# Moving operands of the MLP and of one score product begin past a 256-byte boundary

## The chip, the cores and the metric

The kernel runs on one core of a Trainium2 chip, in one launch. The metric is the device time of that core in microseconds (us), the median of three runs.

## The reference, cut to what matters

Three parts follow each other. Attention without softmax on 8 batches of 3072 rows, an MLP with `h - tanh(h)`, and a top-1 mixture of 8 experts over all 24,576 rows:

```python
scores = (1.0 / S) * np.matmul(z, z.transpose(0, 2, 1))   # z: 8 x 3072 x 64
attn = np.maximum(scores, 0.0) ** 2
x = (u * np.matmul(attn, v)).reshape(B * S, D)            # D = 256
h = x @ w_in                                              # 256 x 2048
x = (h - np.tanh(h)) @ w_out                              # 2048 x 256
logits = x @ w_gate                                       # 8 experts, argmax picks one per row
out[mask] = gate_w * eom * (np.maximum(x[mask] @ w1[e], 0.0) @ w2[e])
```

All data is float32.

## The kernel before, in words

Every float32 operand is split into a rounded part (dtype `float32r`, `fp32r` in the profile) and the rest, so that a product takes three matmuls: high by high, low by high, high by low. A matmul reads a moving operand (here mostly 128 partitions x 512 columns, 2048 bytes of each partition) past a weight block of 128 x 128 that an instruction of its own, LDWEIGHTS, has loaded. Every matmul here has its own LDWEIGHTS, loaded while the matmul before it runs.

The 24,576 rows are worked in 48 chunks of 512 rows. In the attention and MLP stage, three things of three chunks run interleaved in an order that is written out by hand (`at(time, function, ...)` puts a task at a due time, `flush` sorts them, and each engine gets its instructions in that order):

- Scores of chunk c (`s_mm`, 12 steps of 4 matmuls). `t1` holds z transposed, the rounded part in partitions 0 to 63 and the rest in 64 to 127; `t4` is the same with the halves swapped, made by two DMAs from `t1` on SP's queue (`t4_make`, lines 299 to 305). Line 347 multiplies by `t1` as moving operand, line 348 by `t4`; the weights are slices of `t1` in both.
- Attention times v (`av_mm`, lines 382 to 384): the moving operand is `a`, the weights are slices of `v`.
- The MLP of an earlier chunk: `wi_mm` (line 412) has `x` as moving operand and slices of `ws` as weights; `g_first`, `g_second` and `g_third` make `g` from its result; `wo_mm` (lines 451 to 453) has `g` as moving operand and other slices of `ws` as weights. `x` is written once a chunk by `x_make` (lines 391, 392), `g` eight times a chunk by lines 438 and 439. The tile `g` also carries the weights of the MLP while they are split at the start (`w_hi`, `w_lo`).

Then comes the expert stage (`w1_mm` line 851, `w2_mm` lines 889 to 900), whose moving operands are `xt` and `b1`.

Tiles lie in SBUF in pools, in the order in which the pools are opened, and in a pool in the order in which the tags are first met; each tile begins at the next multiple of 32 bytes. In the program before, `x` begins at byte 53248 of each partition, the two buffers of `g` at 63488 and 71680, the two of `t4` at 149504 and 151552, `ws`, `v`, `t1`, `a`, `xt`, `b0`, `b1` and `hh` likewise at multiples of 256; within a tile the halves and slices that a matmul reads begin at multiples of 512. One larger tile does not begin on such a boundary: `rows` begins at 22080, which is 64 bytes past one. It is lent to the splitting of the MLP's weights (`w_conv`, lines 238 to 243, and `w_hi`, line 247) for the even ones of eight steps; the odd ones use the tile `x2`, at 45056, a multiple of 256. Both are named `wk`. The last pool of the attention stage ends at 228352 bytes. At its end the stage's pools close, and the pools `c2` and `c3` of the expert stage take their place.

Of the kernel before, what the change touches and what calls it, by code (L numbers as in the profile page):

```python
# [6 lines left out]
F32R = mybir.dt.float32r  # L7
# [10 lines left out]
P = 128  # L18
FLOOR = 2.0**-15
CH = 512  # L20
# [42 lines left out]
def build(tc, u, v, z, w_in, w_out, w_gate, w_ogate, w1, w2, out):  # L63
# [86 lines left out]
    with ExitStack() as st:  # L150
# [3 lines left out]
        p1, p2, p3 = sp("p1", 1), sp("p2", 2), sp("p3", 3)  # L154
        pva = sp("pva", 1)
        ps_s, ps_h, ps_a, ps_x = pp("ps_s", 1), pp("ps_h", 1), pp("ps_a", 1), pp("ps_x", 1)
        pair = lambda pool, tag, name: pool.tile([P, 2, CH], F32, tag=tag, name=name)

        KEEP = (NG, 0, 1, 2)
# [7 lines left out]
        sa = lambda name, bufs: att.enter_context(tc.tile_pool(name=name, bufs=bufs))  # L167
        a1, a2 = sa("a1", 1), sa("a2", 2)
        pvb, pt, a3 = sa("pvb", 1), sa("pt", NG + 1), sa("a3", 3)

        def fills(zero):

            half = TBL // P // 2
            fill = p1.tile([P, 2, 2, CH], F32R, tag="x2", name="fill").bitcast(I32)
            fill = fill.rearrange("p a d f -> p (a d f)")[:, 0:half]
            nc.gpsimd.memset(fill, N)
            tf = table.rearrange("(p k) o -> p (k o)", p=P)
            for h in range(2):
                nc.sync.dma_start(tf[:, h * half : (h + 1) * half], fill)

            for r in range(N - (2 * CH if NA else 0), N + P, P):
                nc.sync.dma_start(x2d[r : r + P, :], zero)
# [60 lines left out]
            stt(ki, L, 29, ki, op0=ALU.logical_shift_right, op1=ALU.bitwise_or)  # L243

        def w_hi(fp):
            hl = p2.tile([P, 2, 2, CH], F32R, tag="g", name="whl")
            nc.scalar.activation(hl[:, :, 0], WS["k", fp], AF.Copy)
            WS["hl", fp] = hl

# [49 lines left out]

        def t4_make(c):  # L300
            t1 = T1[divmod(c, NG)]
            t4 = a2.tile([P, CH], F32R, tag="t4", name="t4")
            nc.sync.dma_start(t4[0:64, :].bitcast(F32), t1[64:128, :].bitcast(F32))
            nc.sync.dma_start(t4[64:128, :].bitcast(F32), t1[0:64, :].bitcast(F32))
            T4[c] = t4
# [80 lines left out]
        def x_make(c):  # L386
            xf = UT.pop(c)
            for d in range(2):
                nc.vector.tensor_mul(xf[:, d], AVP[c][d], xf[:, d])
            x = p1.tile([P, 2, 2, CH], F32R, tag="x", name="x")  # L390
            nc.scalar.activation(x[:, 0], xf, AF.Copy)
            nc.vector.tensor_sub(x[:, 1], xf, x[:, 0].bitcast(F32))  # L392
            X[c] = x
            del AVP[c]
# [38 lines left out]
        def g_third(c, f):  # L433
            d, s, q, m = HH.pop((c, f))
            nc.vector.scalar_tensor_tensor(q, s, pk, q, op0=ALU.add, op1=ALU.mult)  # L435
            nc.vector.copy_predicated(q, m.bitcast(U16), d)  # L436
            gg = p2.tile([P, 2, 2, CH], F32R, tag="g", name="g")
            nc.vector.tensor_copy(gg[:, 0], q)  # L438
            nc.vector.tensor_sub(gg[:, 1], q, gg[:, 0].bitcast(F32))  # L439
            GG[c, f] = gg  # L440
# [160 lines left out]
        for fp in range(NFP):  # L601
            t = K["C0"] + K["C1"] * fp
            at(t - K["WL"], w_load, fp, 0)
            at(t - K["WL"], w_load, fp, 1)
            for which in range(2):
                at(t + which * K["C1"] / 2, w_conv, fp, which)
            at(t + K["CA"], w_hi, fp)
            at(t + K["CP"], w_lo, fp)
# [5 lines left out]
        for c in range(NCH):  # L614
            t0 = c * TC
            at(t0 - (14 if c else 45), t4_make, c)
            at(t0 + TC / 4, u_load, c)
            at(gap(c, K["UT"] * NJP // 12), u_tr, c)
            for p in range(NJP):
# [4 lines left out]
                at(t + LA, av_mm, c, p)  # L624
            end = c == NCH - 1
            at(t0 + TC + LA + 3.0 + K["XM"] if end else t0 + (TC - DJ) + LA + 3.0, x_make, c)
            tm0 = t0 + TC + LA + K["M0"]
            for f in range(NFP):
                t = tm0 + f * DF
                at(t - 22, ws_load, c, f)  # L630
                for i in range(2):
                    at(t + i * K["HI"], wi_mm, c, f, i)
                    lag = K["LG"] * DF + i * K["HI"]
                    if c == NCH - 2 and f == NFP - 1:

                        lag = tm0 + TC + K["W7"] + 0.1 * i - t
                    at(t + lag, wo_mm, c, f, i)
                at(t + K["HI"] + 1.5, g_first, c, f)
                at(t + K["HI"] + K["G2"], g_second, c, f)
                at(t + K["HI"] + K["G3"], g_third, c, f)  # L640
# [5 lines left out]
            n = int((te + 4.0 - EX - t0) // DJ) + 1  # L646
# [349 lines left out]
        n = nc.values_load(nhb[0:1, 0:1], min_val=0, max_val=NHB)  # L996
# [30 lines left out]
```

## Time and profile before

| | us |
|---|---|
| median of three runs | 5693.54 (5691.28 to 5694.91) |
| the profiled execution | 5712.59 |
| its span, first to last instruction | 5710.8 |

The profile is of one execution. PE is TensorE's matmuls, PEld its weight loads, which run beside them; DVE, ACT and POOL are the vector, scalar and GpSimd engines, SP the engine that issues most DMAs. A matmul's recorded duration (0.39 us for 512 columns) holds the time until its result is out, and the next one begins long before that; how fast matmuls follow each other is read from their start times. The granted clock is a share of the full 2.4 GHz.

### The profile page before, as it was taken

The page shows a single profiled execution, that of the slowest core. Times are in us where ns is not written, and L with a number is a line of the kernel's source. Part 1 is how long each engine was busy: PE and PEld are TensorE (multiplying, and loading weights), DVE is VectorE, ACT ScalarE, POOL GpSimd, SP SyncE. Part 2 cuts the span into 40 slices and gives each one's busy share as a digit, 9 for nine tenths or more (in the row PEclk, how much of TensorE's full clock was granted, in tenths as well). Part 3 has the DMA queues.
Part 4 walks back from the last instruction along what each step waited for, and adds up shares of the span by engine and source line. Part 5 has one row for each costly group of instructions (what it writes and reads, how often), then busy time and mean ns, then how long its engine had stood idle before and what let it go on. Part 6 is the DMA issues. An engine that isn't in the chain of part 4 may idle for free. (4 is left out here: it accounts for less than half of the span.)

```text
span 5710.8 us, 70891 instructions
## 1 busy us (share of the span) xinstructions
PE 5603.9 (98%) x26788; PEld 4644.6 (81%) x26788; DVE 4214.3 (74%) x5091; ACT 3570.7 (63%) x3927; POOL 1795.4 (31%) x1169
## 2 busy tenths in 40 slices
PE   7999999999999999999999999999999999999999
PEld 5888888788888888888888888888887888888898
DVE  7888888888888888888888888888888533333344
ACT  5767776777777777677767776777766422222344
POOL 2224222332333233223322332242222233333355
PEclk9999999999999999999999999999999999999999
DMA  5333333333433333343333433343333566666688
GB/s 203 106 128 135 121 130 123 141 127 125 134 127 125 124 136 125 130 129 136 125 127 120 140 127 122 125 143 111 105 112 118 208 228 224 224 223 224 217 293 288
DMA packets 194007, 872.05 MB, mean 153 GB/s; under 512 B 37178, under 2 KB 78272, under 8 KB 130176
## 3 DMA queue, kind: packets, MB, share of 16 engines
q1 hardware_dynamic: 158080, 769.87, 39.3%
q0 software_dynamic: 35584, 97.63, 4.9%
q8 instruction: 213, 3.49, 0.3%
q14 instruction: 130, 1.06, 0.1%
HBM read 757.16 MB, written 98.96 MB: 150 GB/s over the span
## 5 line engine op out<-in xcount | busy, mean ns | idle before, releaser
L367 POOL TENSOR_TENSOR a<-r,a 128x1024 fp32r<-128x1024 f32 x328 | 789.1, 2406 | 2608.9 <-DVE a L364 2608.5
L353 ACT ACTIVATE r<-sc 128x1024 f32<-128x1024 f32 x576 | 587.2, 1019 | 943.3 <-PE sc L348 936.3
L412 PE MATMUL h<-x,ws 128*128 128x512 f32 x4608 | 1157.5, 391 | 15.8 <-DVE x L392 8.1
L412 PEld LDWEIGHTS h<-x,ws 128*128 128x128 f32 x4608 | 860.4, 188 | 199.5 <-DVE x L392 11.5
L383 PE MATMUL av<-a,v 128*128 128x512 f32 x2304 | 903.8, 392 | 12.2 <-DVE a L367 8.0
L382 PE MATMUL av<-a,v 128*128 128x512 f32 x2304 | 905.1, 393 | 2.1 <-ACT a L362 1.1
L384 PE MATMUL av<-a,v 128*128 128x512 f32 x2304 | 901.2, 391 | 0.0
L863 DVE SCALAR_TENSOR_TENSOR hh<-h,hh 128x1024 fp32r<-128x1024 f32 (+1 forms) x248 | 254.7, 1027 | 722.6 <-ACT hh L862 589.8
L862 ACT ACTIVATE hh<-h 128x1024 fp32r<-128x1024 f32 (+1 forms) x248 | 215.2, 868 | 745.3 <-PE h L851 594.4
L851 PE MATMUL h<-xt,b 128*128 128x512 f32 (+1 forms) x2976 | 610.8, 354 | 20.1 <-DVE xt L834 15.9
L354 ACT ACTIVATE r<-r 128x1024 f32<-128x1024 f32 x576 | 611.4, 1061 | 18.3
L452 PE MATMUL x<-g,ws 128*128 128x512 f32 x1536 | 606.5, 395 | 9.9 <-DVE g L439 7.9
L451 PE MATMUL x<-g,ws 128*128 128x512 f32 x1536 | 606.0, 395 | 6.1 <-DVE g L438 6.1
L420 DVE TENSOR_TENSOR gd<-h,gd 128x1024 f32<-128x1024 f32 x384 | 468.9, 1221 | 180.1 <-ACT gs L419 177.2
L453 PE MATMUL x<-g,ws 128*128 128x512 f32 x1536 | 600.7, 391 | 0.0
L851 PEld LDWEIGHTS h<-xt,b 128*128 128x128 f32 x2976 | 478.6, 188 | 113.7 <-DVE xt L834 27.5
L435 DVE SCALAR_TENSOR_TENSOR gq<-gt,gq 128x1024 f32<-128x1024 f32 x384 | 517.8, 1349 | 52.6 <-ACT gt L430 28.3
L364 DVE CAST a<-r 128x1024 fp32r<-128x1024 f32 x470 | 336.9, 717 | 289.3 <-ACT r L354 177.3
L436 DVE COPY_PREDICATED gq<-gm,gd 128x1024 f32<-128x1024 uint16 x384 | 518.9, 1351 | 13.2
L383 PEld LDWEIGHTS av<-a,v 128*128 128x128 f32 x2304 | 435.7, 189 | 105.6 <-DVE a L367 11.4
L382 PEld LDWEIGHTS av<-a,v 128*128 128x128 f32 x2304 | 435.5, 189 | 95.4 <-ACT a L362 3.5
L384 PEld LDWEIGHTS av<-a,v 128*128 128x128 f32 x2304 | 435.4, 189 | 91.8
(154 smaller groups left out, 9930.8 us busy)
## 6 DMA issues: line engine op xcount, KB each, us to landing
ws<-wsd SPq DMA_DIRECT2D x384, 1024.0 KB
b<-wsp SPq DMA_DIRECT2D x102, 2048.0 KB
wsp<-el POOLq DMA_DIRECT2D x32, 1024.0 KB
x2d<-rows SPq DMA_DIRECT2D x48, 576.0 KB
wr<-in_moe_w SPq DMA_DIRECT2D x25, 1024.0 KB
vr<-in_v SPq DMA_DIRECT2D x48, 512.0 KB
ur<-in_u SPq DMA_DIRECT2D x48, 512.0 KB
er<-in_moe_w SPq DMA_DIRECT2D x32, 512.0 KB
```

The lines of the kernel that those rows point to most:

```text
L353: nc.scalar.activation(r, RR.pop((c, p)), AF.Relu, scale=1.0 / S)
L354: nc.scalar.activation(r, r, AF.Square)
L367: eng.tensor_tensor(a[:, 1], r, a[:, 0].bitcast(F32), op=ALU.subtract)
L382: nc.tensor.matmul(dst, vh, a[:, 0, k], start=(J == 0), stop=False)
L383: nc.tensor.matmul(dst, vh, a[:, 1, k], start=False, stop=False)
L384: nc.tensor.matmul(dst, vl, a[:, 0, k], start=False, stop=(J == 2 * NJP - 1))
L412: nc.tensor.matmul(ps, w, xx, start=(n == 0), stop=(n == 5))
L436: nc.vector.copy_predicated(q, m.bitcast(U16), d)
L451: nc.tensor.matmul(dst, wh, gg[:, 0, i], start=first, stop=False)
L452: nc.tensor.matmul(dst, wh, gg[:, 1, i], start=False, stop=False)
L453: nc.tensor.matmul(dst, wl, gg[:, 0, i], start=False, stop=last)
L851: nc.tensor.matmul(ps[:, j], w, xx, start=(n == 0 and (W == CH or j == 0)), stop=(n == 3 * ND - 1), skip_group_check=W < CH,)
```

## The change

Three tiles get spare columns, and the part that is used begins some columns into the tile. `off(pool, tag, n, k, pad)` takes a tile of n + k + pad columns and returns the n columns from k on.

```diff
+        def off(pool, tag, n, k, pad):
+
+            return pool.tile([P, n + k + pad], F32R, tag=tag, name=tag)[:, k : k + n]
+
+        p4 = sa("p4", 2)
...
         def w_hi(fp):
-            hl = p2.tile([P, 2, 2, CH], F32R, tag="g", name="whl")
+            hl = off(p2, "g", 4 * CH, 8, 8).rearrange("p (a d f) -> p a d f", a=2, d=2)
...
-            t4 = a2.tile([P, CH], F32R, tag="t4", name="t4")
+            t4 = off(p4, "t4", CH, 4, 28)
...
-            x = p1.tile([P, 2, 2, CH], F32R, tag="x", name="x")
+            x = off(p1, "x", 4 * CH, 16, 16).rearrange("p (a d f) -> p a d f", a=2, d=2)
...
-            gg = p2.tile([P, 2, 2, CH], F32R, tag="g", name="g")
+            gg = off(p2, "g", 4 * CH, 8, 8).rearrange("p (a d f) -> p a d f", a=2, d=2)
```

By the order of the pools `x` then begins 64 bytes past a multiple of 256, the two buffers of `g` 160 and 224 bytes, and the two of `t4`, which move to a pool `p4` opened after all others of the stage, 16 and 144 bytes. The spare bytes of `x` (128) and of the two `g` (64 each) add to 256, and those of the two `t4` (128 each) too, so that the other large tiles move by multiples of 256 and their weights stay on the boundary. No instruction, no DMA and no order of instructions is changed.

## Rows read from the trace of the kernel before

**Rows 1.** The page, busy time and share by engine; granted clock in 40 slices.
```profile
PE 5603.9 (98%) x26788; PEld 4644.6 (81%) x26788; DVE 4214.3 (74%) x5091; ACT 3570.7 (63%) x3927; POOL 1795.4 (31%) x1169
...
PEclk9999999999999999999999999999999999999999
```

**Rows 2.** Busy time by stretch: stretch, its length, busy us and instructions by engine.
```profile
200.00:3200.00 3000.00, 2984.03 (x13645) 2453.53 (x13644) 2538.38 (x2920) 2147.69 (x2282) 911.50 (x504) 1.00 0.37 128
```

**Rows 3.** Who PE waited for: us in total, times, longest.
```profile
PE h L851 <- DVE xt L834: 15.9, 32, 2.6
PE h L412 <- DVE x L392: 8.1, 8, 1.1
```

**Rows 4.** Groups on PE by line and shape: count, busy us, mean ns, idle before.
```profile
L412 PE MATMUL h<-x,ws 128*128 128x512 f32 x4608 | 1157.5, 391 | 15.8 <-DVE x L392 8.1 <-DVE gq L422 5.8 <-issue 1.7
...
L452 PE MATMUL x<-g,ws 128*128 128x512 f32 x1536 | 606.5, 395 | 9.9 <-DVE g L439 7.9
L451 PE MATMUL x<-g,ws 128*128 128x512 f32 x1536 | 606.0, 395 | 6.1 <-DVE g L438 6.1
L453 PE MATMUL x<-g,ws 128*128 128x512 f32 x1536 | 600.7, 391 | 0.0
...
L348 PE MATMUL sc<-t,t 128*128 128x512 f32 x1152 | 449.9, 391 | 0.0
```

**Rows 5.** Timeline of PE, an even stretch: start us, duration us, what.
```profile
1011.75 0.39 PE L383 MATMUL av<-a,v 128*128 128x512 f32 x1
...
1016.28 0.40 PE L453 MATMUL x<-g,ws 128*128 128x512 f32 x1
```

**Rows 6.** Timeline of PE where transposes of u follow.
```profile
977.03 1.52 PE L412 MATMUL h<-x,ws 128*128 128x512 f32 x6
978.39 1.07 PE L333 MATMUL ups<-ident,ur 128*128 128x128 f32 x8
```

**Rows 7.** Timeline of the weight loads of the same stretch.
```profile
976.81 1.32 PEld L412 LDWEIGHTS h<-x,ws 128*128 128x128 f32 x6
978.37 0.86 PEld L333 LDWEIGHTS ups<-ident,ur 128*128 128x128 f32 x8 [0.24 <-issue]
```

**Rows 8.** Timeline of PE, an uneven stretch after four short matmuls.
```profile
1017.11 0.39 PE L383 MATMUL av<-a,v 128*128 128x512 f32 x1
...
1017.57 0.40 PE L382 MATMUL av<-a,v 128*128 128x512 f32 x1
1017.81 0.39 PE L383 MATMUL av<-a,v 128*128 128x512 f32 x1
...
1019.42 0.39 PE L384 MATMUL av<-a,v 128*128 128x512 f32 x1
```

**Rows 9.** The tile `wk`: shortest/median/longest ns, first and last start, form.
```profile
L241 DVE TENSOR_SCALAR wk<-wk x16: 426/427/429, 19.8 to 115.3; 128x512 int32<-128x512 int32 x16
L242 DVE SCALAR_TENSOR_TENSOR wk<-wraw,wk x16: 691/693/694, 20.2 to 115.7; 128x512 int32<-128x512 int32 x16
...
L247 ACT ACTIVATE whl<-wk x8: 1037/1056/1067, 27.1 to 117.2; 128x1024 fp32r<-128x1024 f32 x8
```

**Rows 10.** The lines that write `x` and `g`: shortest/median/longest ns.
```profile
L391 ACT ACTIVATE x<-ut x48: 1040/1043/1062, 95.9 to 4423.1; 128x1024 fp32r<-128x1024 f32 x48
...
L392 DVE TENSOR_TENSOR x<-ut,x x48: 1225/1226/2603, 97.0 to 4424.2; 128x1024 fp32r<-128x1024 f32 x48
...
L438 DVE CAST g<-gq x384: 693/694/1080, 112.5 to 4526.2; 128x1024 fp32r<-128x1024 f32 x192
...
L439 DVE TENSOR_TENSOR g<-gq,g x384: 1224/1226/1643, 113.2 to 4527.0; 128x1024 fp32r<-128x1024 f32 x192
```

**Rows 11.** Timeline: the DMAs that make a `t4` on SP, its first reader on PE.
```profile
1091.88 0.49 SPq L303 DMA_DIRECT2D t<-t  x1
1092.42 0.65 SPq L304 DMA_DIRECT2D t<-t  x1
...
1103.15 0.39 PE L348 MATMUL sc<-t,t 128*128 128x512 f32 x1
```

## The prediction

> **What bounds the kernel now.** I read the page's busy shares first, then the busy times of a long middle stretch, then PE's waits, PE's groups, and last the start times of single matmuls. PE is busy 98% of the span at a full granted clock, the 2.4 GHz level [rows 1]. Between 200 and 3200 us it is busy 2984 of 3000 us, while DVE has 2538 (85%) and ACT 2148 (72%) [rows 2]. Its waits are small: the two longest entries of the whole run are 15.9 and 8.1 us [rows 3]. So the stage lasts as long as PE's matmuls follow each other, and only a change of their step can move the time by much.
>
> The step is read from start times. In an even stretch from 1011.75 to 1016.28 us there are 21 matmuls of 512 columns (lines 382 to 384, 347, 348 and 451 to 453 in turn), so 20 steps in 4.53 us: 226.5 ns [rows 5]. Line 412 has the same step: six from 977.03 until the next instruction at 978.39 make 226.7 ns [rows 6]. At 2.4 GHz, 512 columns at one a cycle are 213.3 ns, so each matmul pays 13.3 ns, 32 cycles, above its columns. All the operands in these stretches begin on a multiple of 256 bytes.
>
> **The change part by part.** It adds and removes no instruction. It moves the start of what 10,368 matmuls read: line 412 with 4608, lines 451 to 453 with 3 x 1536 = 4608, line 348 with 1152 [rows 4]. The 6912 matmuls of lines 382 to 384, and line 347, are untouched.
>
> (1) The step of these 10,368. No row shows a moving operand of this size off a boundary, so I bound it. Below: the whole 13.3 ns could be two readers of SBUF, the moving operand and the next weights, in each other's way because both begin on the same boundary, and the offset could free them: 10,368 x 13.3 ns = 138 us less. Above: in an uneven stretch single steps are as long as 0.24 us (1017.57 to 1017.81), 13.4 ns above the even step [rows 8]; with that on every one, 139 us more. I take 0, because the nearest row speaks against a clash. The last of the six matmuls of line 412 begins at 977.03 + 5 x 0.227 = 978.16. The last weight load before it begins at 976.81 + 5 x 0.227 = 977.94, ends at 976.81 + 1.32 = 978.13, and the next one begins at 978.37; the row gives 0.24 us without any load [rows 7]. So this matmul has no weight load beside it for 0.21 us, practically all of its columns, and still the next one begins 0.23 us after it, the common step. The same pattern comes in 47 of the 48 chunks, with a step of 226 or 227 ns. The 32 cycles are then paid by the matmul itself, and where its operand begins relative to other weights is no part of them.
>
> The Trainium skill, "TensorE: Matmul & The Clock Gate", section "Wait — 56ns, not 53.3ns?", gives 215.7 ns for back-to-back matmuls of 512 columns at the full clock. The trace's 226.5 ns is 10.8 ns above that; if an offset brought every changed matmul to the page's figure, that would be an estimated 112 us less. The page names no alignment as the condition, and no run here shows its figure.
>
> (2) The writers. `x` is written by lines 391 and 392, `g` by lines 438 and 439, now at 64, 160 and 224 bytes past a boundary. The tile `wk` tells what that costs: half of its 16 instructions on line 241 and on line 242 work on a tile 64 bytes past a boundary and half on one that is on it, and shortest and longest are 426 and 429 ns, 691 and 694 ns; on ACT 1037 and 1067 ns for 8 [rows 9]. Were a writer slower by ACT's whole spread, 3%, line 439 would take 37 ns more of its 1226 [rows 10], 384 times 14 us of DVE, and DVE has 15% of the stage free [rows 2]. Cost 0. If that cover were gone, PE's waits for `x` and `g` (8.1 us for line 392, 7.9 and 6.1 us for lines 439 and 438 [rows 3, 4]) would grow, by at most those 14 us.
>
> (3) `t4` and the DMAs. Its two DMAs are issued at 1091.88 and 1092.42, the first matmul that reads the tile begins at 1103.15: 10.7 us of slack [rows 11]. PE's idle time ahead of line 348 is 0.0 [rows 4]. A slower landing, or a double one, stays inside. By the skill's "DMA: Bandwidth & Descriptors", section "How a descriptor splits into AXI transactions", a row of 2048 bytes that begins off a 256-byte boundary takes 9 pieces instead of 8, an estimated eighth more; no run here shows it.
>
> (4) The pools. The large tiles behind shift by multiples of 256 bytes, and `t4` leaves the middle of the stage for its end, so the expert stage's `b` and `hh` tiles come to lie over other tiles of the attention stage (over `v`, `a` and `t1` where they lay over `t4` and `r`). The last readers of all these are the last chunk's matmuls, which end before the expert stage's fetches are due: 0, at most a wait of some us once.
>
> Sum: 0 against the profiled execution's 5712.59 us (span 5710.8). That execution is 0.33% above the median of the runs, 5693.54; I forecast against the median, 5693.5 us.
>
> **The rivals.**
> A, the offset breaks the even step; slower. The step is not always 226.6 ns: after four short matmuls it runs 231.0 ns (10 steps from 1017.11 to 1019.42) before it settles [rows 8]. So some timing between the reads of SBUF and the array does count, in units of a few cycles, and a moving operand that begins inside a unit of reading could need one more read each time. Place: every matmul of lines 412, 451 to 453 and 348, or those at 160 and 224 and at 16 and 144 alone. Price: 4.4 ns x 10,368 = 46 us, 5739; for the `g` and `t4` lines alone (5760) 25 us, 5719; at the bound of 139 us, 5832. It decides from about 1.1 ns a matmul on (11 us). For it: nothing is known of starts inside 256 bytes. Against: the uneven stretch has operands on the boundary, so its cause is the short matmuls before it, not the start.
> B, the offset frees a clash; faster. If 32 cycles were a clash of the two reads, 138 us less: 5556; if half of it, 69 us: 5624; DVE's 15% would cover it, since the stage would shrink by at most 138 of some 4300 us. For it: the two streams begin together, the load 0.00 to 0.01 us after the matmul, on the same boundary. Against: rows 6 and 7, where no load runs and the step stays.
> C, PE's step stays and a writer or a DMA gets slower. It would show as PE waits on `x`, `g` or `t4`; at the 14 us of (2), 5708. Little speaks for it.
>
> **How the numbers follow.** A measurement of this kernel can tell about 0.2%, 11 us, from no change. Forecast, no change: 0.64, own range 5682 to 5705. A: 0.20 (0.12 at 20 to 50 us, 0.08 from there to the bound). B: 0.13 (0.10 at 50 us and more). C: 0.03, half of it above 11 us. So faster 0.13, same 0.66 (0.64 and what of A and C stays under 11 us), slower 0.21. The range leaves out B's larger half and more, some 0.10, and A from the 46 us upward with its margin, some 0.08: 5650 to 5745.
>
> **What would show it.** After the change: lines 412, 451 to 453 and 348 in an even stretch still step at 226 to 227 ns, the same as lines 382 to 384, which serve as the control within the same trace; lines 391, 392, 438 and 439 keep 1043, 1226, 694 and 1226 ns [rows 10]; nothing waits on `t`. A shows as a longer step on the changed lines and an unchanged one on lines 382 to 384, and by line it tells which offset costs: 64 on 412, 160 and 224 on 451 to 453, 16 and 144 on 348. B shows as a step towards 213 ns on the changed lines. My forecast is wrong if any of these lines moves by more than about 1 ns a matmul.

## The result and the profile after

The changed kernel takes 5734.57 us (5732.40 to 5738.97, three runs) against 5693.54: ratio 1.0074 with the 95% interval 1.0051 to 1.0097, so 41 us slower. The forecast was no change, its own range 5682 to 5705; the time that came lies near rival A's 5739.

The page of the kernel after, answering to [rows 1]: as many instructions, PE 42 us busier, the other engines' busy time the same within 7 us, the granted clock full as before.

```profile
PE 5645.9 (99%) x26788; PEld 4640.9 (81%) x26788; DVE 4211.7 (73%) x5091; ACT 3568.9 (62%) x3927; POOL 1802.4 (31%) x1169
...
PEclk9999999999999999999999999999999999999999
```

Busy time by stretch after, answering to [rows 2]: in the same 3000 us PE gets through 13,516 matmuls instead of 13,645, 0.95% fewer, and its busy time is not less. It is the pace that fell, not the supply.

```profile
200.00:3200.00 3000.00, 2988.25 (x13516) 2429.72 (x13515) 2513.70 (x2894) 2128.47 (x2263) 905.50 (x497) 1.00 0.37 127
```

PE's waits after (us in total, times, longest), answering to [rows 3], with the lines of the new file (6 higher): none is new, and those on `x` and `g` are no longer than before.

```profile
PE h L418 <- DVE x L398: 7.2, 8, 1.0
...
PE x L458 <- DVE g L445: 5.8, 11, 0.8
PE x L457 <- DVE g L444: 5.8, 2, 3.5
```

The timeline of PE after (start us, duration us), answering to [rows 5, 6]. In one stretch: lines 457 to 459 go from 1021.70 to 1024.27 in 11 steps of 233.6 ns, line 418 from 1015.29 to 1018.03 in 12 steps of 228.3, lines 353 and 354 from 1014.36 to 1015.29 in 4 steps of 232.5. In the stretches read before, these lines stepped at 226.5 to 226.7 [rows 5, 6]. The untouched lines 388 to 390 right behind the displaced `x` go from 1018.03 to 1018.96 in 4 steps of 232.5, and from 1018.96 to 1020.78 in 8 of 227.5: they too lose some ns in their first matmuls and then recover.

```profile
1014.36 0.39 PE L353 MATMUL sc<-t,t 128*128 128x512 f32 x1
...
1015.29 2.91 PE L418 MATMUL h<-x,ws 128*128 128x512 f32 x12
1018.03 0.39 PE L388 MATMUL av<-a,v 128*128 128x512 f32 x1
...
1018.96 0.39 PE L389 MATMUL av<-a,v 128*128 128x512 f32 x1
...
1020.78 0.39 PE L353 MATMUL sc<-t,t 128*128 128x512 f32 x1
...
1021.70 0.40 PE L457 MATMUL x<-g,ws 128*128 128x512 f32 x1
...
1024.27 0.40 PE L459 MATMUL x<-g,ws 128*128 128x512 f32 x1
```

Over the whole run, the mean steps (of those up to 250 ns, from the start times of all matmuls) are, before and after: line 412 with `x` 227.1 and 230.6; lines 451 to 453 with `g` 227.5 and 233.7; line 348 with `t4` 226.8 and 230.7; line 347, untouched, 226.7 and 230.3; lines 382 to 384, untouched, 227.2 and 228.3. Times the number of matmuls of each line, the longer steps make 16 us on line 412, 29 on lines 451 to 453, 4.5 on line 348, 4 on line 347 and 7 on lines 382 to 384: 61 us. Steps above 250 ns, where PE waited for something, are 73 fewer, and what they hold above the line's mean step shrinks by 21 us: a slower PE is waited for instead of waiting. The two make 40 us.

The writers, answering to [rows 10], keep their medians, 1043, 694 and 1226 ns.

```profile
L397 ACT ACTIVATE x<-ut x48: 1040/1043/1068, 95.0 to 4462.0; 128x1024 fp32r<-128x1024 f32 x48
L444 DVE CAST g<-gq x384: 693/694/1077, 111.5 to 4562.7; 128x1024 fp32r<-128x1024 f32 x192
L445 DVE TENSOR_TENSOR g<-gq,g x384: 1224/1226/1645, 112.2 to 4563.4; 128x1024 fp32r<-128x1024 f32 x192
```

The two profiled spans differ by 20 us only. The profiled execution of the kernel before ran some 19 us longer in the expert stage, which the change does not touch, than the executions it was timed with, and so did those of `all64`, `ws64` and `mlp64` below, beside which the kernel before takes 5715.84 us. The length of the attention and MLP stage is therefore read from the last time that `x` is written: 4424.2 before [rows 10], and after

```profile
L398 DVE TENSOR_TENSOR x<-ut,x x48: 1224/1226/2597, 96.0 to 4463.1; 128x1024 fp32r<-128x1024 f32 x48
```

38.9 us later, nearly the whole of the 41.

### The profile page after: what moved, and what is told of

Read it like the earlier page. It is cut to its first block, busy times and chain, and to the rows that moved or that the text cites. A ratio compares the mean times of both kernels' runs of the same rounds, so it can differ in the third digit from the quotient of the medians.

```text
span 5730.7 us, 70891 instructions
## 1 busy us (share of the span) xinstructions
PE 5645.9 (99%) x26788; PEld 4640.9 (81%) x26788; DVE 4211.7 (73%) x5091; ACT 3568.9 (62%) x3927; POOL 1802.4 (31%) x1169
## 5 line engine op out<-in xcount | busy, mean ns | idle before, releaser
L418 PE MATMUL h<-x,ws 128*128 128x512 f32 x4608 | 1173.6, 395 | 13.4 <-DVE x L398 7.2
L457 PE MATMUL x<-g,ws 128*128 128x512 f32 x1536 | 614.7, 400 | 5.8 <-DVE g L444 5.8
L458 PE MATMUL x<-g,ws 128*128 128x512 f32 x1536 | 613.7, 400 | 6.4 <-DVE g L445 5.8
L459 PE MATMUL x<-g,ws 128*128 128x512 f32 x1536 | 609.5, 397 | 0.0
```

The source lines that it names most:

```text
L418: nc.tensor.matmul(ps, w, xx, start=(n == 0), stop=(n == 5))
L457: nc.tensor.matmul(dst, wh, gg[:, 0, i], start=first, stop=False)
L458: nc.tensor.matmul(dst, wh, gg[:, 1, i], start=False, stop=False)
L459: nc.tensor.matmul(dst, wl, gg[:, 0, i], start=False, stop=last)
```

## The experiments

Three theories. **T**: a moving operand that begins off a 256-byte boundary costs by itself. **R**: what counts is the distance between the starts of the moving operand and of the weights loaded beside it. **S**: each product runs well alone, and the loss is in switching between operands of different starts.

### The parts of the change

Each part alone, the other operands back on the boundary (`t4` in its new pool in all three):

```diff
 x_only:  x = off(p1, "x", 4 * CH, 16, 48)    g: off(..., 0, 0)   t4: off(p4, "t4", CH, 0, 0)
 g_only:  x = off(p1, "x", 4 * CH, 0, 32)     g: off(..., 8, 8)   t4: off(p4, "t4", CH, 0, 0)
 t4_only: x = off(p1, "x", 4 * CH, 0, 0)      g: off(..., 0, 0)   t4: off(p4, "t4", CH, 4, 28)
```

> x alone begins 64 bytes past a boundary; g and t4 on it (t4 in its new pool). The profile after the change has line 418 at a mean step of 230.6 ns against 227.1 before, so 4608 x 3.5 ns = 16 us of the 41 us: 5710 us, ratio 1.0028. T, R: the step of the line that multiplies x is 230 to 231 ns, lines with g back at 227.5. S: less than a third of the whole, under 5705, because fewer switches remain.

> g alone begins 160 and 224 bytes past a boundary; x and t4 on it. The profile after the change has the three lines with g at 233 to 234 ns against 227.5 before, so 4608 x 6.2 ns = 29 us: 5722 us, ratio 1.0050. T, R: these lines at 233 to 234 ns, the line with x back at 227. S: under 5712.

> t4 alone begins 16 and 144 bytes past a boundary; x and g on it. The profile after the change has line 354 at 230.6 ns against 226.8 before, and its neighbour, line 353, whose operand begins on the boundary, at 230.3: T: 1152 x 3.9 ns = 4 us, 5698, ratio 1.0008, and line 353 back at 227. R and S: 2304 x 3.7 ns = 9 us, 5702, ratio 1.0015, with line 353 still above 229.

Measured against 5693.24 for the kernel before, timed beside them: `x` alone 5715.11, ratio 1.0040 (1.0026 to 1.0053); `g` alone 5721.49, 1.0049 (1.0035 to 1.0063); `t4` alone 5703.18, 1.0018 (1.0009 to 1.0027). The last write of `x` begins at 4444.3, 4448.6 and 4434.0, so 20, 24 and 10 us later than before.

The three times are near what was expected; `x` is 6 us dearer. S as the only cause is out, since `x` alone and `g` alone cost more than it allows. T and R both stand, and `t4` alone does not part them: its time is that of R and S, but line 353, which they wanted above 229 ns, is back at 227.3.

The parts add to 54 us of stage, the whole has 38.9. Worked out as above, the longer steps on the displaced lines themselves do add up: 15.5, 28 and 5 us in the parts, 49 in the whole. What does not add up is the lines that a part left on the boundary: they cost 16, 8 and 10 us more in the parts, but only 11.5 in the whole. With `x` alone lines 388 to 390 rise from 227.2 to 228.6 and lines 353 and 354 to 229.0; with `t4` alone the line with `x` rises to 228.5. So a displaced operand also slows its neighbours, and the sum of the parts counts some of this more than once.

### The product alone

A kernel of matmuls alone, 32 for each pair of starts, tells T from R:

```diff
+ nc.tensor.matmul(ps[k % 2], w[:, wo // 4 : wo // 4 + 128], m[:, mo // 4 : mo // 4 + 512], ...)
```

> Leaves out the whole computation: it only runs groups of 32 matmuls (128x512 float32r, one weight load each) into one PSUM bank, a group for each of 22 starts of the moving operand (0 to 512 bytes past a 256-byte boundary) and 8 starts of the weights (0 to 256 bytes past one), and writes a tile to the output. R (what counts is the distance between the start of the moving operand and that of the weights loaded beside it): 226.7 ns a step wherever both begin at the same distance past a boundary (0/0, 16/16, 64/64, 128/128, 192/192), 230 to 235 ns where they differ. T (a moving operand that begins off a 256-byte boundary costs by itself): 226.7 ns at 0, 256 and 512 whatever the weights, 230 to 235 ns elsewhere. S (the single product doesn't care; the loss in the full kernel comes from switching between operands with different starts): 226.7 ns everywhere.

Steps in ns, the mean of the last 23 of each group (the first group, 0 and 0, begins at the lower clock, with steps of 427 ns, and is left out), for 13 of the starts:

| moving / weights | 0 | 16 | 32 | 64 | 96 | 128 | 192 | 256 |
|---|---|---|---|---|---|---|---|---|
| 16 | 231.5 | 231.1 | 236.8 | 234.7 | 233.5 | 233.3 | 230.9 | 231.6 |
| 32 | 233.3 | 228.3 | 226.7 | 233.4 | 233.2 | 234.3 | 233.1 | 233.3 |
| 48 | 233.4 | 233.3 | 231.6 | 226.7 | 234.6 | 233.5 | 230.8 | 233.4 |
| 64 | 228.9 | 231.7 | 233.3 | 226.7 | 233.4 | 233.2 | 232.3 | 228.9 |
| 80 | 231.2 | 226.7 | 233.4 | 231.6 | 226.7 | 234.6 | 233.3 | 231.2 |
| 96 | 233.4 | 230.2 | 228.9 | 233.3 | 226.7 | 233.4 | 234.1 | 233.4 |
| 112 | 231.1 | 233.3 | 231.2 | 233.4 | 231.6 | 226.7 | 233.2 | 231.1 |
| 144 | 233.3 | 233.6 | 231.1 | 231.2 | 233.4 | 231.5 | 234.8 | 233.3 |
| 160 | 234.3 | 233.3 | 233.1 | 233.4 | 228.9 | 233.3 | 233.4 | 234.3 |
| 192 | 233.2 | 232.2 | 234.3 | 233.2 | 233.4 | 228.9 | 226.7 | 233.2 |
| 224 | 233.4 | 233.4 | 233.2 | 234.3 | 233.1 | 233.4 | 233.3 | 233.4 |
| 240 | 226.7 | 226.7 | 234.6 | 233.5 | 233.3 | 231.1 | 233.4 | 226.7 |
| 256 | 226.7 | 226.7 | 233.4 | 233.3 | 234.3 | 233.2 | 228.9 | 226.7 |

T is out: with the moving operand on the boundary and the weights at 32 the step is 233.4, and with both at 32 it is 226.7. R holds where the weights begin at a multiple of 32: equal distances give equal steps, within 1.4 ns for starts that are multiples of 16, at all distances but one. At distance 0 the step is the even one; with the moving operand 64 bytes ahead it is 228.9, at most other distances 231 to 235. Starts of 0 and of 256 for the weights give the same columns, so what counts repeats after 256 bytes.

Two things do not fit R. At the one distance, the moving operand 16 bytes behind the weights (240 and 256, 48 and 64, 80 and 96), the step is 226.7 too in six of seven such pairs, and 236.8 in the seventh (16 and 32). And with the weights at 16, R's own pair of 16 and 16 runs at 231.1, while 80, 128, 176 and 240 run at 226.7. So equal starts are not the only pairs with the even step. No group of all 176 is below 226.65. In the timeline (start us, duration us of 32 matmuls) the groups with the moving operand at 224, 240 and 256 and weights on the boundary begin at 127.94, 135.40 and 142.66: 7.46 us, then 7.26, 233 and 227 ns a matmul; the second of these, 240 and 0, is one of the pairs with the moving operand 16 bytes behind.

```profile
127.94 7.62 PE L39 MATMUL pa<-m,w 128*128 128x512 f32 x32
135.40 7.42 PE L39 MATMUL pb<-m,w 128*128 128x512 f32 x32
142.66 7.45 PE L39 MATMUL pa<-m,w 128*128 128x512 f32 x32
```

For the changed kernel the column 0 says: 4608 at 228.9, 2304 each at 234.3 and 233.4, 576 each at 231.5 and 233.3, against 226.7: 10.1 + 17.5 + 15.4 + 2.8 + 3.8 = 49.6 us. The kernel's own steps on these lines make 49 us, but line by line they differ: 3.5 ns on the line with `x` where the map says 2.2, 6.2 on those with `g` where it says 7.2 on average.

### Starts in the full kernel

`all64` puts 64 unused bytes ahead of all tiles, `ws64` displaces only the weights of the MLP, `mlp64` these weights with `x` and `g`:

```diff
 all64:  +    const.tile([P, 16], F32, name="skip")      # ahead of bias_b
 mlp64:  +    p1.tile([P, 16], F32, tag="skip")          # ahead of x; rest of 192 bytes behind ws
 ws64:   +    2 x p2.tile([P, 8], F32, tag="skip")       # behind g; rest of 192 bytes behind ws
```

> The kernel before with 64 unused bytes ahead of all tiles: every tile, moving operands and weights alike, begins 64 bytes further, so none of the large ones is on a 256-byte boundary and all distances are as before. R (the distance between the start of the moving operand and that of the weights loaded beside it counts): the even step stays 226.7 ns, 5693 us, within 6. T (a moving operand off the boundary costs by itself): all 18,432 matmuls of 512 columns in the first stage pay some 3.5 ns or more, 65 us: over 5750.

> Only the weights ws begin 64 bytes past a boundary; all moving operands are on it, as before. R: the lines with x and g step at 229 to 234 ns, 9216 x 2.3 to 6.7 ns = 21 to 62 us, less what the longer steps save of waits: 5712 to 5745. T: 5693.

> x, g and also their weights ws begin 64 bytes past a boundary; t4, t1, a and v on it. R: inside the MLP's groups the distance is 0 again and the step 226.7 ns; only the matmul at the border of two groups has weights of another start beside it (about 32 borders a chunk at 4 to 6 ns, 48 chunks: 6 to 9 us): 5697 to 5706. T: as with x and g displaced alone, 9216 matmuls at 3.5 ns or more: over 5722.

Timed beside these, the kernel before took 5715.84 us. `all64`: 5717.34, ratio 1.0001 (0.9992 to 1.0010). `ws64`: 5761.81, 1.0081 (1.0067 to 1.0095), 46 us slower with every moving operand on the boundary. `mlp64`: 5742.86, 1.0048 (1.0034 to 1.0061), 27 us. The last write of `x` in `all64`, then `ws64`, then `mlp64`, against 4424.2:

```profile
L393 DVE TENSOR_TENSOR x<-ut,x x48: 1215/1226/2600, 97.2 to 4425.3; 128x1024 fp32r<-128x1024 f32 x48
```
```profile
L395 DVE TENSOR_TENSOR x<-ut,x x48: 1224/1226/2602, 96.1 to 4469.9; 128x1024 fp32r<-128x1024 f32 x48
```
```profile
L394 DVE TENSOR_TENSOR x<-ut,x x48: 1224/1226/2596, 96.1 to 4451.7; 128x1024 fp32r<-128x1024 f32 x48
```

`all64` and `ws64` refute T in the kernel itself: all operands off the boundary cost nothing, the weights alone off it cost as much as the whole change. With `ws64` the lines with `x` and `g` step at 232.8 and 233.2 ns; the map has 233.3 for this pair (256 and 64). `mlp64` missed R's 4 to 13 us. Its steps by place in a group of the MLP's matmuls show why R is not all: the first ten take 225 to 236 ns, 231 on average, and only the eleventh and twelfth are at 226.9 and 226.8. Most groups are six long and end before that. The untouched lines 382 to 384 take 230.4, 232.6, 230.8 and 228.5 in their first four and 226.8 from the ninth on. So S has a share: switching starts costs, on both sides of the switch.

### Switching and state

> Leaves out the whole computation: groups of 48 matmuls as in the first map. A, 16 starts of the moving operand with weights on the boundary, in three orders, the third with four short matmuls ahead of each group: if the step depends on the starts alone, each start has one step in all orders, 226.7 at 0 and more at most others; if the state that the engine comes from decides, they differ between orders. B, both operands at one start, then the weights 16 bytes behind and ahead: R says 226.7 for equal starts, all 16 of them. C, starts that change from matmul to matmul, 0 and 32, 64, 160 or 224: if the weights loaded beside a matmul count, the second group of each pair (its own weights at the other start, the next ones at its own) is at 226.7 and the first group is not; if its own weights count, the other way round; D and E, 2x256 columns followed by 256, and 256 alone, as in the expert stage: whether any start is below the 351 ns a pair and the 120 ns of now. No step of 512 columns below 226.

Both operands at one start (first matmul to next group, 48 matmuls): at 0, 16 and 32 the groups begin at 551.88, 562.77 and 573.81 and the fourth at 584.74: 226.9, 230.0 and 227.7 ns a matmul, the last of these with its first nine steps uneven (225 to 236 ns), as in `mlp64`. Behind their first eight steps all eight starts that are multiples of 32 run at 226.7 to 226.8, and all eight odd multiples of 16 at 230.0 to 230.1.

```profile
551.88 11.05 PE L52 MATMUL pa<-m,w 128*128 128x512 f32 x48
562.77 11.21 PE L52 MATMUL pb<-m,w 128*128 128x512 f32 x48
573.81 11.09 PE L52 MATMUL pa<-m,w 128*128 128x512 f32 x48
584.74 11.21 PE L52 MATMUL pb<-m,w 128*128 128x512 f32 x48
```

Starts that change from one matmul to the next, 0 with 32, 64, 160 or 224: 231.6, 231.7, 233.9 and 231.6 when each has its own weights at its own start, 230.0, 231.6, 230.0 and 230.0 when it has the next one's weights there. Neither reaches 226.7, so "beside it" in R is not shown; alternating itself costs 3 ns and more. And the state counts. With the weights 16 bytes ahead of the moving operand all 16 pairs of part B run at 233.3, 240 and 0 among them, which has 236.6 to 236.7 in the three orders of part A; in the first map, run on another chip, six of seven such pairs have 226.7. The pair 112 and 0 ran at 231.1, 226.7 and 231.1 in the three orders. The other 14 starts of part A off the boundary repeat within 1.1 ns.

Two matmuls of 2x256 and 256 columns, as in the expert stage, take 353.5 ns a pair at 0 and 346.7 with the moving operand at 16, 32, 160 or 224 (the 356.7 and 349.5 of the next expectation are means with one wide matmul too many, some 3 ns high); 256 columns alone 120.0 at 0 and 113.3 at 112 and 192. The boundary is not the best start for every order.

### The best starts of the expert stage

> Leaves out the whole computation: the order of the expert stage's matmuls (12 of 512 columns, 8 pairs of 2x256 and 256; then 12 of 256 columns, 4 such pairs; four times each) for 8 starts of xt by 8 starts of b1 (0 to 224 bytes in steps of 32), weights on the boundary. R with the single steps of the second map: at 0 and 0 the first sort takes 12 x 226.7 to 231 + 8 x 351 to 356.7 = 5.53 to 5.63 us, the best (xt at 0, b1 at 32, 160 or 224) 5.52; the second sort 12 x 120 + 4 x 356.7 = 2.87 us at 0 and 0 and 12 x 113.3 + 4 x 349.5 = 2.76 at xt 192 and b1 224. S: switching between starts eats that, and 0 and 0 is within 0.5% of the best.

From start to start, the first sort of group takes 5593 ns at 0 and 0, 5507 with `b1` at 160, 5527 with `b1` at 32; the second 2851, 2824 and 2813. (The figures of the next two expectations leave out one short step and are 28 and 8 ns higher; their differences are the same.) By 39 and 23 blocks of four groups `b1` at 160 saves 16 us, about the best of the 64 pairs. So S's half a percent was too little: 5507 is 1.5% below. Then the kernel before with only this changed:

```diff
+ t = cp[2].tile([P, 2 * NF2 * D + 64], F32R, tag="b1", name="b1")[:, 40 : 40 + 2 * NF2 * D]   # b1_32: 8
```

> The kernel before with one change in the expert stage: b1, the moving operand of its second product, begins 160 bytes past a boundary, everything else on it. The third map has 5.534 us for the first sort of group against 5.621 at 0 and 0 (39 blocks of 4 groups: 13.6 us less) and 2.833 against 2.859 for the second (23 blocks: 2.4 us less): 16 us, 0.28% less than the kernel before on the same chip, if starts decide inside the kernel as they do alone. S: the stage's waits and short matmuls set the state anyway, and less than 5 us comes out, ratio 0.9991 or more.

> The same with b1 32 bytes past a boundary: 5.553 against 5.621 (10.6 us) and 2.821 against 2.859 (3.5 us): 14 us less, ratio 0.9975. S: ratio 0.9991 or more.

Against 5693.79 for the kernel before, timed beside them, `b1` at 160 takes 5682.79, ratio 0.9981 (0.9972 to 0.9990), at 32 it takes 5683.49, 0.9982 (0.9973 to 0.9991). Both are faster than the kernel before, by 11 and 10 us where the map said 16 and 14. A stretch of the expert stage in the profile of `b1` at 160, PE busy throughout, holds 1559 matmuls:

```profile
4900.00:5200.00 300.00, 300.00 (x1559) 254.47 (x1558) 99.65 (x130) 88.51 (x117) 101.98 (x104) 1.00 0.66 231
```

and in that of the kernel after, whose expert stage is that of before and runs without the extra 19 us, 1542 (and 1542 again 39 us on, at the same place of the stage):

```profile
4900.00:5200.00 300.00, 300.00 (x1542) 251.51 (x1541) 99.27 (x130) 87.08 (x115) 102.02 (x104) 1.00 0.65 226
```

Over the expert stage's matmuls (lines 851 and 889 to 900) the steps of up to 300 ns add to 1103 us in both profiles with `b1` moved and to 1114 in those of the kernel after and of the three parts, while the longer ones, with waits, hold 43 to 45 us in all of them. So the 11 us are PE's pace again. The 512-column matmuls of line 851, whose own operands stayed on the boundary, go from 230.7 to 231.1 ns there to 227.8 and 228.1: in this order too, a start acts on its neighbours.

## Why the prediction was wrong

**The bound** was right: PE's step sets the stage, and its 0.95% fewer matmuls in 3000 us are the loss.

**Step (1), the step of the 10,368 matmuls, failed.** It took 0 because a matmul with no weight load beside it keeps the 226.7 ns [rows 6, 7]. That reading holds for what it tests: the 32 cycles above the columns are no clash that an offset could free, and no pair of starts went below 226.65. But it bears on the gain alone. From there the prediction went on to "where its operand begins relative to other weights is no part of them" and took 0 for both sides, though about a start that is worse the rows said nothing. `all64` and `ws64` and the maps show what stands in its place: the even step is the best case. With starts at multiples of 32 it is held while moving operands and weights begin at the same distance past 256 bytes, and the other distances cost 2.2 ns (64 bytes) to some 8 ns, plus the switches. The term that was put at 0 measures 38.9 us in the stage: 61 us of longer steps, 49 on the displaced lines and 11.5 on the others, less 21 that waits give back.

**The control failed.** Lines 382 to 384, which the prediction named as the control in the same trace, rose by 1.1 ns and line 347 by 3.5, so the trace held no undisturbed line to compare with. The steps by place show the rise in the first matmuls behind a switch.

**Steps (2) to (4) held**: the writers' medians are the same, no matmul waits for `t4`'s DMAs (the waits on `t`, 3.4 and 0.7 us on ACT, are those of before), and no wait is new. The new pool of `t4` was not run alone with nothing else changed; it is part of all three partial kernels.

**Rival A**, at a chance of 0.20, had the sign, and its 46 us lie near the measured 41. That nearness is partly luck. The price came from an uneven stretch with every operand on the boundary [rows 8], 4.4 ns on each changed matmul. The displaced lines rose by 3.5, 6.2 and 3.9 ns, lines that A left alone rose as well, and waits gave a third back. Its reason, a start inside a unit of reading, is not borne out: with all tiles moved by 64 bytes nothing is lost. Only starts at odd multiples of 16 cost 3.3 ns even when equal. **Rival B** is refuted for this change, since no pair of starts in the first map runs below the step of the boundary. **Rival C** did not come.

The Trainium skill, "TensorE: Matmul & The Clock Gate", section "Step-by-step: what each phase is for", describes the two reads, moving operand and weights, as independent ports. Here the step depends on the distance between their starts (`ws64`: 46 us with the weights alone displaced), so in time they are not independent. What they share is not settled by any run, nor what state makes one pair of starts run at two paces.

## What to carry to other kernels

When a row shows that a cost cannot shrink, it has not shown that it cannot grow: test each side with its own row, and give that side a price from the nearest disturbed stretch, here 231.0 instead of 226.6 ns, knowing that its cause may be another. For matmuls of 512 columns, let moving operands and weights that run in turn begin at the same distance past a 256-byte boundary, at a multiple of 32, and treat a padding tile as a change of pace, not of layout alone. Where the order mixes lengths, a map of starts in that very order, one short kernel, is cheaper than reasoning and gave a faster version.

## What the runs showed of the hardware

- The start of an operand modulo 256 bytes moves the pace of back-to-back matmuls of 512 columns between 226.65 and about 237 ns, at a full granted clock and with nothing waited for.
- Equal starts at multiples of 32 bytes run at 226.7 ns once settled, equal starts at odd multiples of 16 at 230.0 (second map).
- The same pair of starts can run at two paces in one run, 231.1 and 226.7 ns for 112 and 0, 236.7 and 233.3 for 240 and 0 (second map), where only what ran before differs.
- After a switch of starts the first nine or ten matmuls can take 225 to 236 ns before the step is even again (`mlp64`, second map).
- 256 columns alone run at 120.0 ns with all starts on the boundary and at 113.3 with the moving operand at 112 or 192: there equal starts are not the best.
